# Two fewer steps in a reciprocal square root, scales found by integer steps, column sums accumulated in PSUM, and a new written order

## The chip, the cores and the metric

The kernel runs on one core of one Trainium2 chip, in one launch. The metric is the device time of that launch in microseconds (us). Lower is better. Five engines share the work, each with its own queue that is served in order: TensorE (PE) multiplies matrices, VectorE (DVE) and ScalarE (ACT) do elementwise work and reductions, GpSimd (POOL) builds a few constants at the start, and SyncE (SP) issues the transfers. An engine that reaches an instruction whose input is not there yet waits, and everything behind it on that engine waits too.

## The reference

The program is an attention layer followed by two layers of matrix products, all on 2304 tokens of width 512.

```python
scores = scale * np.matmul(q, k.transpose(0, 1, 3, 2))      # q, k, v: 4 x 8 x 576 x 64
mask_plain = (rel >= 0) & (rel < window)                    # heads 0 to 3, window 32
mask_dil = (rel >= 0) & (rel < window * dilation) & (rel % dilation == 0)   # heads 4 to 7
attn = softmax(np.where(masks, scores, -1e9)); x = np.matmul(attn, v)

h = x @ w_in                                                # 512 -> 1024
solu = h * softmax(h)
ln = (solu - mu) / np.sqrt(var + 1e-06) * g_ln              # mean and variance over the 1024
x = ln @ w_out                                              # 1024 -> 512

h = x @ w_in2                                               # 512 -> 2048
g = np.maximum(h, 0.0) + np.log1p(np.exp(-np.abs(h)))       # softplus
out = g @ w_out2                                            # 2048 -> 512
```

(`softmax` stands here for the reference's own lines: subtract the row's maximum, take the exponential, divide by the sum.)

## The kernel before

**Numbers as pairs.** Most products are made in 16-bit floats from operands that are split in a high and a low half, so one product of the reference is three on PE (high by high, high by low, low by high). Before a tensor is split it is scaled by a power of two that is near the root mean square of the whole tensor. There are 14 such scales: one each for the two weights of the first layer (`w1i`, `w1o`), one for each quarter of the two weights of the second (`w2i0` to `w2i3`, `w2o0` to `w2o3`), and one set of three (for q, k and v) for each of the four batches (`pre0` to `pre3`).

**How a scale is found.** ACT squares the tensor piece by piece and leaves one column of 128 partial sums per piece (8 pieces for a first-layer weight, 4 for a quarter, 9 columns for a batch, or 3 in `pre0`, which needs v alone). PE then multiplies a 128 x 128 matrix of ones in 32-bit floats by all those columns at once, which adds over the partitions. The operations of PE are named `w1im`, `w2o1m`, `pre1m` and so on. DVE adds the columns up (`tensor_reduce`), and the four steps of `scale_of` take the maximum with a tiny number, clear the mantissa by two shifts, take the reciprocal and multiply it. Only then can the tensor be split.

**The attention** goes through 28 pairs of blocks, `n` = 0 to 27, seven for each batch; the two blocks of a pair are written n.0 and n.1. The first ten pairs work in 32-bit floats and turn their operands on PE (`tq`, `tk`, `tp`, `tx`); the other eighteen work in split 16-bit floats and turn them by transposing transfers. In both, `QK` is the product of scores, `PV` the product with the values. Between `QK` and `PV` of a late block stand, in this order: the mask with its maximum on DVE (`mx`), four exponentials on ACT (`ex`), the split into high and low half (`ph`, `pl`), and a transposing transfer (`pT`).

**The first layer** has 18 tiles of 128 tokens. `m1a` and `m1b` are its products (12 each). Behind them a chain of DVE and ACT steps makes the gated and normalised tile. In that chain the reciprocal square root of the variance is found on DVE alone with numbers of one column (`m1k`): a first guess by integer steps on the bit pattern, and then refinements. Its result goes through a transposing transfer, and `ya`, `yb` multiply it by the second weight, 24 products each.

**The second layer** has, for each group of 256 tokens, eight products `h` (24 matrix products each) and eight products `o` (12 each), with the softplus between. The groups 5 to 8 are taken in two twins that save one product in eight by sums of the weights (operations `P`).

**What sets the order.** No scheduler decides it. Every operation is recorded with its engine choices, and a long table of numbers (`ORDER`) gives the sequence in which the operations are written out, with the engine of those that could run on either DVE or ACT; a second table (`SLOTS`) gives the buffers. A negative number in `ORDER` stands for a **fill**: a product of the unit matrix by itself into a PSUM bank that is free at that place, 128 x 512 in 16-bit floats, whose result nobody reads. The functions that the change touches are printed here with the line numbers of the profile. In them `ts`, `stt`, `recip` are DVE instructions on one or a few columns, `mm` is one product on PE, and `P.chain` records steps of which each waits for the one ahead.

Of the kernel before, what the change touches and what calls it, by code (L numbers as in the profile page):

```python
# [144 lines left out]
def kernel(  # L145
# [12 lines left out]
    nc = tc.nc  # L158
# [32 lines left out]
        65, 66, 247, 248, 278, 277, 0, 13, -2, -2, -2, 250, 252, 2943, 3, 2945, 14, 67, 69, -2, -2, 280, 254, 281,  # L191
        1, 255, 266, 267, 256, 15, 16, 4, 249, 68, -5, -5, -5, -5, -5, -5, -5, 257, 5, 279, 282, 6, 28, 308, 18,
        70, 268, 2, -5, -5, -5, 71, 7, 2975, 2950, 269, 307, 72, 73, 74, 75, 76, 77, 78, -5, 284, 309, 285, 296,
        -5, 259, 270, 17, 260, 286, -5, -5, -5, 287, 288, 261, 29, 2954, 263, 264, 297, 271, 272, 310, 33, 30,
        2965, -5, -5, -5, -5, 313, 38, 274, -5, 298, 367, 314, 299, 19, 20, 31, 32, -5, -5, 315, 275, 21, 22, 3008,
        289, 290, 276, 265, 34, 35, 291, 23, -5, -5, -5, -5, 317, 300, 366, 292, -5, -5, 293, 36, 318, 319, 37,
        301, 39, 40, 302, 41, 303, -5, -5, -5, -5, -5, 320, 321, 294, 24, 25, 26, 8, -5, -5, -5, -5, 304, 305, 42,
        9, 10, 11, -5, 372, 365, 306, 329, 27, 295, 373, 364, 79, 80, 12, -5, -5, -5, -5, -5, -5, -5, -5, -5, -5,
        -5, -5, -5, -5, -5, 43, 44, 45, 46, 311, 368, 312, 47, 48, 330, 81, 2753, 82, 370, 371, 53, 49, -5, -5, -5,
        331, 51, 62, 332, 421, 83, -5, 374, -5, -5, -5, 424, 425, 54, 94, 375, 422, 376, 63, 114, 322, 386, 95,  # L200
        323, 50, 52, -5, 333, 64, 334, -5, -5, 377, 324, 387, 378, -5, -5, -5, -5, -5, -5, 388, 96, 3017, 451, 84,
        426, 369, 59, 389, 115, 109, 423, 427, -5, -5, -5, 326, 97, 335, 60, 57, 327, 428, 336, 328, -5, -5, 337,
        379, 429, 440, 452, 380, 116, 507, 55, 98, 338, 339, 430, 381, -5, -5, -5, -5, -5, -5, -5, 431, 382, 454,
        117, 1163, 56, 432, 110, -5, 383, 58, -5, 433, 142, 99, 111, 112, 85, 455, 390, 118, 441, 508, 384, 391,
        385, 89, 505, 434, 86, 340, 435, 100, 442, 87, 113, 443, 101, 88, 341, 392, 393, 394, 102, 90, 91, 104,
        444, 92, 445, 103, 456, 436, 342, 395, 457, 93, 506, 105, 397, 343, 143, 106, 396, 446, 234, 562, 107, 511,
        437, 344, 347, 144, 513, 398, 512, 345, 563, 453, 438, 439, 108, 346, 458, 235, 447, 448, 177, 145, 348,
        146, 514, 147, 349, 399, 153, 459, 470, 565, 449, 566, 178, 218, 158, 350, 179, 450, 879, 481, 180, 460,
        461, 509, 471, 119, 351, 154, 181, 352, 462, -4, -4, 472, 567, 568, 219, 148, 400, 353, 120, 354, 155, 463,
        355, 121, 356, 156, 357, 122, 464, 358, 157, 465, 473, 515, 474, 159, 359, 160, 123, 232, 360, 220, 161,  # L210
        516, 527, 162, 124, 3053, 517, 518, 149, 125, 3158, 2820, 150, 2828, 475, 528, 233, 529, 129, 151, 519,
        140, 530, 2818, 476, 221, 878, 467, 362, 881, 882, 510, 520, 182, 477, 152, 222, 908, 521, 183, 883, 522,
        184, 132, 884, 224, 187, 478, 479, 3215, 223, 468, -1, 524, 185, 141, 480, 525, 526, 531, 186, 401, 137,
        469, 532, 130, 225, 138, 569, 133, 402, 533, 363, 403, 134, 404, 570, 188, 163, 581, 164, 571, 131, 189,
        226, 165, 139, 405, 582, -6, -6, -6, -6, -6, 583, 572, 534, 535, 135, 192, 909, 228, 227, 230, 910, 127,
        406, 482, 573, 536, 564, 166, 190, 914, 167, 407, 193, 911, 191, 168, 408, 194, 409, 195, 410, 175, 176,
        229, 411, 537, 196, 197, 592, 231, 412, 483, 413, 171, 880, 169, 538, 198, 414, 199, 584, 415, 1160, 173,
        1164, 200, 172, 201, 170, 236, 416, 174, 915, 237, 484, 202, 238, 885, 593, 239, 886, 240, 594, 417, 916,
        597, 203, 418, 241, 595, 539, 242, 917, 1161, 897, 243, 419, 244, 204, 887, 888, 245, 596, 205, 598, 206,
        599, 898, -3, -3, -3, -3, -3, 574, 207, 485, 585, 575, 208, 576, 889, 577, 486, 600, 607, 899, -1, -1, -1,  # L220
        -1, 578, 586, 1171, 209, 487, 587, 588, 488, 601, 900, -1, -1, -1, -1, -1, -1, 589, 579, 1172, 608, 420,
        489, 609, 890, 590, 591, 891, 580, 210, 602, 214, 216, 892, 610, 901, 902, 912, -5, -5, 971, 893, 211, 894,
        903, 611, 490, 1205, 895, 215, 1162, 540, 904, 212, 603, 491, 604, 217, 1212, 605, 492, 896, 213, 972, 606,
        905, 906, 907, 973, 626, 627, 493, 1159, -5, -5, -5, -5, -5, -5, 612, 613, 974, 913, 494, 631, 628, 614,
        495, 629, -5, -5, -5, 918, 496, 919, 497, 615, 967, 930, 616, 498, 617, 246, 499, 630, 3314, 541, 500, 632,
# [1524 lines left out]
```

## Time and profile before

| what | value |
|---|---|
| median of 3 runs | 697.88 us (694.92 to 698.5) |
| the profiled execution | 698.44 us, of which 696.5 us lie between the first and the last instruction (the span) |
| PE busy | 675.2 us, 97% of the span |
| DVE busy | 556.0 us, 80% |
| ACT busy | 480.9 us, 69% |
| mean granted clock of PE | 0.988 of full speed |

The busy share of PE counts fills as work, and the ends of its matrix products are modelled, so one product's duration overlaps the next one's. What a product costs in a row of many is therefore read from the distance between two starts, not from its duration. The shares over the whole span mix two very different stretches: in the first 130 us or so the weights are being split and the attention's first pairs are made, by DVE and ACT above all, and after that there is always a matrix product ready for PE.

### The profile page before, as it was taken

Reading aid. Unit: us, or ns where it says so; the run is one execution under the profiler, and the core shown is the slowest. Engines: PE = TensorE matmul, PEld = TensorE weight load, DVE = VectorE, ACT = ScalarE, POOL = GpSimd, SP = SyncE. Lnnn points to the kernel's source line nnn. Section 1 sums busy time; section 2 is a strip of 40 time slices with the busy share of each in tenths; the row PEclk is TensorE's granted clock in tenths of the full one; section 3 lists DMA queues with packets and bytes.
Section 4 is the critical chain, followed back from the end, with each engine's and each line's share of the span. In section 5 each row is a group of like instructions: output and inputs, shape, how many; then the busy total and the mean of one; then the engine's idle time right before and its main releaser. Section 6 shows DMA issues by size and latency. Waiting matters only on the chain.

```text
span 696.5 us, 14184 instructions
## 1 busy us (share of the span) xinstructions
PE 675.2 (97%) x5223; PEld 463.9 (67%) x5223; DVE 556.0 (80%) x1619; ACT 480.9 (69%) x1015; POOL 3.5 (1%) x22
## 2 busy tenths in 40 slices
PE   7999699999999999999999999999999999999997
PEld 4665547766765588688667668666776668676653
DVE  4999999999999968788889899887887768544233
ACT  4889998999998776987799797976364632322312
POOL 2000000000000000000000000000000000000000
PEclk9999689999999999999999999999999999999999
DMA  9889987669876558989887887652012110000001
GB/s 266 247 233 259 225 225 193 162 170 188 184 147 164 146 176 185 200 162 157 158 152 153 153 162 136 116 113 43 1 31 62 31 31 1 1 32 31 1 1 60
DMA packets 186773, 89.80 MB, mean 129 GB/s; under 512 B 157000, under 2 KB 174416, under 8 KB 186704
## 3 DMA queue, kind: packets, MB, share of 16 engines
q1 hardware_dynamic: 186704, 88.90, 56.4%
q8 instruction: 41, 0.67, 0.4%
q14 instruction: 28, 0.23, 0.1%
HBM read 54.53 MB, written 4.72 MB: 85 GB/s over the span
## 4 chain that ended last, share of the span: by engine, by line
PE 69%; DVE 12%; DMA 10%; ACT 4%; issue 3%; SPq 1%; ACTq 0%; DVEq 0%
PE ps_w L552 31%; PE bank L552 26%; PE bank L1550 11%; DMA xd<-x 2%; DVE E L543 2%; DMA E<-in_v_dram 2%; DMA qT<-qk 1%; DMA pT<-p 1%; DVE W L543 1%; PE bank L558 1%; DVE s L1122 1%; DMA W<-in_moe_w_out_dram 1%; ACT E L534 1%; DMA rv<-in_v_dram 1%; DMA rq<-in_q_dram 1%
## 5 line engine op out<-in xcount | busy, mean ns | idle before, releaser
L552 PE MATMUL ps_w<-W,g 128*128 128x512 f16 x864 | 194.3, 379 | 0.0
L552 PEld LDWEIGHTS <-W 128*128 128x128 f16 x1824 | 176.5, 98 | 23.3 <-DMA lnT<-hl 0.7
L552 PEld LDWEIGHTS <-g 128*128 128x128 f16 x864 | 83.6, 98 | 91.4
L552 PE MATMUL bank<-y,W 128*128 128x256 f16 x960 | 109.9, 273 | 0.0
L552 PE MATMUL ps_w<-W,xr 128*128 128x512 f16 x432 | 99.5, 382 | 1.0 <-ACT xr L534 1.0
L552 PE MATMUL bank<-lnT,W 128*128 128x256 f16 x864 | 98.7, 273 | 0.2 <-DMA lnT<-hl 0.2
L552 PEld LDWEIGHTS <-xr 128*128 128x128 f16 x432 | 42.1, 99 | 46.9 <-ACT xr L534 1.5
L543 DVE SCALAR_TENSOR_TENSOR g<-r,KR,g 128x512 f16<-128x512 f32 x68 | 50.3, 744 | 15.2 <-ACT g L534 14.2
L1718 ACT ACT_TABLE_LOAD x43 | 55.2, 1283 | 0.7
L1550 PEld LDWEIGHTS <-W 128*128 128x128 f16 x480 | 47.0, 98 | 8.4
L534 ACT ACTIVATE E<-E 128x768 f32<-128x768 f32 (+3 forms) x51 | 37.9, 744 | 15.7 <-DVE E L543 8.8
L534 ACT ACTIVATE s<-s 96x128 f32<-96x128 f32 (+3 forms) x144 | 43.5, 374 | 2.4 <-DVE st L538 1.2
L1122 DVE CUSTOM_DVE_ANT_0 s<-bank,band,bsc 96x128 f32<-96x128 f32 (+3 forms) x144 | 38.9, 324 | 3.9 <-PE bank L552 3.6
L534 ACT ACTIVATE r<-bank,invC 128x512 f32<-128x512 f32 x40 | 27.2, 685 | 16.4 <-PE bank L552 15.5
L534 ACT ACTIVATE r<-r,invT 128x512 f32<-128x512 f32 x21 | 14.6, 714 | 32.5 <-DVE r L546 32.4
L534 ACT ACTIVATE xf<-bank,rs 80x64 f32<-80x64 f32 (+1 forms) x128 | 29.3, 314 | 7.2 <-DVE rs L549 4.8
L552 PE MATMUL ps_w<-eye 128*128 128x512 bf16 x108 | 31.4, 407 | 0.7 <-DVE e L543 0.7
L534 ACT ACTIVATE g<-r,KR 128x512 f16<-128x512 f32 x35 | 24.9, 715 | 6.6 <-PE ps_w L552 6.3
L552 PEld LDWEIGHTS <-pT 128*96 128x96 f16 (+3 forms) x432 | 23.1, 123 | 6.9 <-issue 1.5
L543 DVE SCALAR_TENSOR_TENSOR E<-E 128x512 int32<-128x512 int32 x40 | 27.1, 683 | 0.1
L552 PEld LDWEIGHTS <-eye 128*128 128x128 bf16 (+2 forms) x162 | 16.5, 111 | 15.8 <-POOL eye L611 4.0
L534 ACT ACTIVATE hl<-e,st 128x1024 f16<-128x1024 f32 x18 | 22.3, 1242 | 5.4 <-DMA lnT<-hl 3.2
(295 smaller groups left out, 1102.9 us busy)
## 6 DMA issues: line engine op xcount, KB each, us to landing
E<-in_moe_w_in_dram SPq DMA_DIRECT2D x17, 512.0 KB, 4.8
E<-in_moe_w_out_dram SPq DMA_DIRECT2D x17, 512.0 KB, 4.1
out_dram<-osb SPq DMA_DIRECT2D x18, 256.0 KB, 2.4
W<-in_moe_w_in_dram SPq DMA_DIRECT2D x7, 512.0 KB, 5.7
W<-in_moe_w_out_dram SPq DMA_DIRECT2D x7, 512.0 KB, 6.2
E<-in_v_dram SPq DMA_DIRECT2D x9, 384.0 KB, 4.0
E<-in_q_dram SPq DMA_DIRECT2D x9, 384.0 KB, 3.4
E<-in_k_dram SPq DMA_DIRECT2D x9, 384.0 KB, 3.4
```

The costliest lines, as they stand in the source:

```text
L534: pin(nc.scalar.activation(out=out, in_=in_, func=func, **kw))
L543: pin(nc.vector.scalar_tensor_tensor(out=out, in0=in0, scalar=s, in1=in1, op0=op0, op1=op1, **kw))
L552: pin(nc.tensor.matmul(out, l, r, start=start, stop=stop))
L558: pin(nc.tensor.transpose(out, in_, eye32[:in_.shape[0], :in_.shape[0]]))
L1122: pin(nc.vector.tensor_tensor_reduce(out=sv()[:rows, h, :nk], in0=sb.t[:rows, h, :nk], in1=band[:rows, 48 - m:48 - m + nk], scale=sc[:rows ...
L1550: pin(nc.tensor.matmul(ps.t[:, ff, :], at(w, cc, ff), yo.t[:, v, cc, :], start=start, stop=cc == 1 and x == 2, skip_group_check=True,))
L1718: pin(nc.scalar.preload_act_table_set(TABLES[tab]))
```

## The change

There are four parts.

1. **The chain of the root.** The nine one-column steps become seven, in each of the 18 tiles. The first guess is one instruction (a multiplication of the integer by -0.5 and an addition) where it was two, and three refinements of two instructions each become one of three and one of two.
2. **The scales.** The columns of partial sums are no longer multiplied by the ones in one product and then added on DVE. PE makes one 32-bit product with the ones for each column (three for a batch) and accumulates them in PSUM. DVE's `tensor_reduce` goes, and so do the reciprocal and the multiplication, for which one integer step stands (a subtraction of exponents).
3. **Small leftovers.** A copy in each batch's scale, a negative scale that nobody reads, and three of four one-column doublings go.
4. **The order.** `ORDER` and `SLOTS` are new throughout. The four PSUM banks are four separate tiles in both kernels.

```diff
     ORDER = (
-        65, 66, 247, 248, 278, 277, 0, 13, -2, -2, -2, 250, 252, 2943, 3, 2945, 14, 67, 69, -2, -2, 280, 254, 281,
+        232, 236, 231, 234, 235, 63, 64, 261, -2, -2, 264, 265, 2855, 238, 0, 1, 239, 250, 2620, 240, 233, 262, 13,
...
-    def scale_of(inv, sc, ss):
+    def scale_of(inv, sc, ss, uses):
 
         i = sc.bitcast(INT32)
         return [
-            (TINY, lambda e: ts(sc, ss() if callable(ss) else ss, 2.0 ** -80, op0=ALU.max)),
+            (dve_cost(0, x=1), lambda e: ts(sc, ss(), 2.0 ** -80, op0=ALU.max), [], uses),
             (TINY, lambda e: ts(i, i, 24, 23, ALU.logical_shift_right, ALU.logical_shift_left)),
-            (TINY, lambda e: recip(inv, sc)),
-            (TINY, lambda e: ts(inv, inv, 2.0 ** -50)),
+            (TINY, lambda e: ts(inv.bitcast(INT32), i, -1.0, float((254 - 50) << 23), ALU.mult, ALU.add)),
         ]
...
-        m = P.op(f"pre{b}m", pe_cost(0.15), lambda e: mm(pb.t[:, 3 * c0:9], ones, am[:, 3 * c0:9], True, True), after=parts, uses=[pb])
...
+        def total(e):
+            for x in range(3):
+                mm(pb.t[:, c0:3], ones, am[:, 3 * c0 + x:9:3], x == 0, x == 3 - 1)
+
+        m = P.op(f"pre{b}m", pe_cost(0.2), total, after=parts, uses=[pb])
...
         pb = Buf(ps_x)
-        m = P.op(f"{name}m", pe_cost(0.15), lambda e: mm(pb.t[:, 0:n], ones, am[:, 0:n], True, True), after=squares, uses=[pb])
+        cols = list(range(n))
+
+        def total(e):
+            for i in cols:
+                mm(pb.t[:, 0:1], ones, am[:, i:i + 1], i == cols[0], i == cols[-1])
+
+        m = P.op(f"{name}m", pe_cost(0.06 + 0.06 * len(cols)), total, after=squares, uses=[pb])
...
-            (TINY, lambda e: pin(nc.vector.tensor_reduce(out=t[:, 0:1], in_=pb.t[:, 0:n], axis=AXX, op=ALU.add)), [], [pb]),
-            *scale_of(inv, sc, t[:, 0:1]),
+            *scale_of(inv, sc, lambda: pb.t[:, 0:1], [pb]),
...
             lambda e: ts(col(7), col(6), 1.0 / F1, 1e-6, ALU.mult, ALU.add),
-            lambda e: ts(i32(9), i32(7), 1, op0=ALU.logical_shift_right),
-            lambda e: ts(i32(9), i32(9), -1.0, float(0x5F3759DF - 2 ** 31), ALU.mult, ALU.add),
+            lambda e: ts(i32(9), i32(7), -0.5, float(0x5F3759DF - 2 ** 31), ALU.mult, ALU.add),
             lambda e: stt(col(10), col(9), col(9), col(7), ALU.mult, ALU.mult),
-            lambda e: stt(col(9), col(10), 3.0, col(9), ALU.subtract, ALU.mult),
+            lambda e: stt(col(8), col(10), 10.0 / 3.0, col(10), ALU.subtract, ALU.mult),
+            lambda e: stt(col(9), col(8), 5.0, col(9), ALU.add, ALU.mult),
             lambda e: stt(col(10), col(9), col(9), col(7), ALU.mult, ALU.mult),
-            lambda e: stt(col(9), col(10), 12.0, col(9), ALU.subtract, ALU.mult),
-            lambda e: stt(col(10), col(9), col(9), col(7), ALU.mult, ALU.mult),
-            lambda e: stt(col(10), col(10), 768.0, col(9), ALU.subtract, ALU.mult),
+            lambda e: stt(col(10), col(10), 64.0 / 3.0, col(9), ALU.subtract, ALU.mult),
```

**Where the order moves, on PE, at the sum of a quarter's squares.** The place is `w2o1m`, the sum for the second quarter of the last weight, some 134 us into the span. `amw_83` holds the columns of partial sums, `bank_137` the result, `y` and `xr` are the operands of the products ahead and behind. Before:

```order
947 L552 MATMUL bank_139<-y_123,W 128x256
948 L552 LDWEIGHTS eye
949 L552 MATMUL ps_w_140<-eye 128x512
950 L552 MATMUL bank_137<-amw_83,ones 128x4
951 L552 LDWEIGHTS xr
952 L552 MATMUL ps_w_140<-W,xr 128x512
```

The same place after:

```order
925 L547 MATMUL bank_139<-y_123,W 128x256
926 L547 LDWEIGHTS eye
927 L547 MATMUL ps_w_140<-eye 128x512
928 L547 MATMUL bank_137<-amw_83,ones 128x1 x4
929 L547 LDWEIGHTS xr
930 L547 MATMUL ps_w_140<-W,xr 128x512
```

One product of four columns has become four products of one column; the fill ahead of it and the first-layer tile behind it stand where they stood. The same happens at the other 13 sums. Counted over the whole order, the products with the ones go from 14 to 60, and the fills from 142 to 127.

**On DVE, at the last scale.** `s2o` is the scale of the last quarter, `tmp_91`, `invC`, `invD`, `iD` and `KR` are the factors made from it. Before:

```order
618 L738 TENSOR_REDUCE tmp_90<-bank_137 128x1
619 L538 TENSOR_SCALAR s2o<-tmp_90 128x1
620 L540 TENSOR_SCALAR s2o<-s2o 128x1
621 L549 RECIPROCAL s2o<-s2o 128x1
622 L538 TENSOR_SCALAR s2o<-s2o 128x1
623 L543 SCALAR_TENSOR_TENSOR invC<-s2i,s1o 128x1
```

After:

```order
566 L533 TENSOR_SCALAR s2o<-bank_137 128x1
567 L535 TENSOR_SCALAR s2o<-s2o 128x1 x2
568 L538 SCALAR_TENSOR_TENSOR invC<-s2i,s1o 128x1
569 L535 TENSOR_SCALAR tmp_91<-invC 128x1
570 L538 SCALAR_TENSOR_TENSOR tmp_91<-tmp_91,s2o 128x1
```

Five instructions have become three, the first of them reading PSUM.

**On PE, in the middle of the attention, ahead of `PV21.0`.** `pT` is the transposed matrix of weights that the transfer brings, `v` the values; `lnT` by `W` is `ya4.1`. Before, the 24 products of `ya4.1` stand between the scores of pair 22 (`kT`) and `PV21.0`; the first and the last of them are shown here:

```order
5067 L552 MATMUL bank_136<-kT,qT 80x80
5068 L552 LDWEIGHTS W
5069 L552 MATMUL bank_138<-lnT_122,W 128x256
...
5114 L552 LDWEIGHTS W
5115 L552 MATMUL bank_138<-lnT_122,W 128x256
5116 L552 LDWEIGHTS pT
5117 L552 MATMUL bank_137<-v_111,pT 80x65
```

After:

```order
5036 L547 LDWEIGHTS E
5037 L547 MATMUL bank_136<-kT,E 80x80
5038 L547 LDWEIGHTS pT
5039 L547 MATMUL bank_137<-v_111,pT 80x65
...
5061 L547 MATMUL bank_137<-v_111,pT 80x65
5062 L547 LDWEIGHTS W
5063 L547 MATMUL bank_139<-lnT_122,W 128x256
```

`PV21.0` now follows the scores directly, and `ya4.1` comes behind it.

## Rows read from the trace of the kernel before

**Rows 1.** Busy time by stretch: engine busy (instructions), granted PE clock, DMA share, GB/s.
```profile
5.00:64.00 59.00, 58.76 (x450) 37.61 (x449) 53.32 (x130) 45.93 (x149) 0.00 (x0) 1.00 0.95 259
64.00:72.00 8.00, 7.05 (x61) 4.40 (x59) 7.41 (x29) 8.00 (x23) 0.00 (x0) 1.00 0.83 259
72.00:94.00 22.00, 15.59 (x86) 10.44 (x86) 20.61 (x56) 20.84 (x62) 0.00 (x0) 0.61 0.97 241
94.00:131.00 37.00, 35.80 (x299) 25.86 (x298) 35.65 (x118) 33.20 (x93) 0.00 (x0) 1.00 0.74 184
131.00:300.00 169.00, 167.49 (x1311) 116.26 (x1309) 152.64 (x477) 146.15 (x297) 0.00 (x0) 1.00 0.74 172
300.00:430.00 130.00, 127.48 (x1155) 93.53 (x1154) 114.33 (x420) 108.92 (x203) 0.00 (x0) 1.00 0.83 155
430.00:683.00 253.00, 253.00 (x1830) 171.70 (x1828) 168.61 (x391) 115.21 (x194) 0.00 (x0) 1.00 0.18 38
```

**Rows 2.** Who PE waited for from 131 us on: us in total, times, longest.
```profile
PE bank L552 <- DMA pT<-p: 1.0, 1, 1.0
PE ps_w L552 <- ACT xr L534: 1.0, 1, 1.0
PE bank L552 <- DMA qT<-qk: 0.9, 2, 0.5
PE bank L552 <- DVE xf L546: 0.5, 1, 0.5
PE bank L552 <- ACT xf L534: 0.4, 1, 0.4
```

**Rows 3.** Groups by line and shape, the fills: count, busy us, mean ns, idle before.
```profile
L552 PE MATMUL ps_w<-eye 128*128 128x512 bf16 x108 | 31.4, 407 | 0.7 <-DVE e L543 0.7
L552 PE MATMUL bank<-eye 128*128 128x512 bf16 x34 | 10.8, 421 | 4.9 <-POOL eye L611 4.0 <-ACT qk L534 0.9
```

**Rows 4.** Chain that ended last, one piece, fifteen fills: start us, us, what.
```profile
29.58 3.24 PE ps_w L552 x15
```

**Rows 5.** The tile of ones: duration ns min/median/max, first and last start, forms.
```profile
L552 PEld LDWEIGHTS bank<-amw,ones x20: 186/190/333, 32.4 to 238.2; 128*128 128x128 f32 x20
L552 PE MATMUL bank<-amw,ones x20: 169/253/373, 32.7 to 238.3; 128*128 128x4 f32 x16, 128*128 128x8 f32 x4
L552 PE MATMUL bank<-am,ones x8: 168/214/257, 15.3 to 315.5; 128*128 128x9 f32 x6, 128*128 128x3 f32 x2
```

**Rows 6.** PE and its weight loads in order of time, around two sums: start, us.
```profile
134.53 0.30 PEld L552 LDWEIGHTS bank<-amw,ones 128*128 128x128 f32 x2 [0.21 <-ACT E L534]
238.25 0.28 PE L552 MATMUL bank<-amw,ones 128*128 128x4 f32 x2
238.39 1.24 PE L552 MATMUL ps_w<-W,xr 128*128 128x512 f16 x5
```

**Rows 7.** PE in order of time, a 32-bit `PV` and the fill behind it.
```profile
126.11 0.82 PE L552 MATMUL bank<-xd,pT 96*96 96x65 f32 x8
126.76 1.03 PE L552 MATMUL ps_w<-eye 128*128 128x512 bf16 x4
128.49 2.78 PE L552 MATMUL bank<-y,W 128*128 128x256 f16 x24
```

**Rows 8.** DVE in order of time, the first and last of six, five of them one-column.
```profile
67.15 0.15 DVE L540 TENSOR_SCALAR st<-st 128x1 int32<-128x1 int32 x1
...
67.67 0.68 DVE L543 SCALAR_TENSOR_TENSOR W<-E,W 128x512 int32<-128x512 int32 x1
```

**Rows 9.** PE in order of time, the scores of block 21.0, `ya4.1` and `PV21.0`.
```profile
368.29 0.47 PE L552 MATMUL bank<-kT,E 128*80 128x80 f16 x8
389.51 2.79 PE L552 MATMUL bank<-lnT,W 128*128 128x256 f16 x24
393.32 0.65 PE L552 MATMUL bank<-v,pT 80*80 80x65 f16 x12 [1.03 <-DMA pT<-p]
```

More of the change, by code (lines that the diff above doesn't have):

```diff
@@ L655, in prepass @@
         pb = Buf(ps_x)
-        m = P.op(f"pre{b}m", pe_cost(0.15), lambda e: mm(pb.t[:, 3 * c0:9], ones, am[:, 3 * c0:9], True, True), after=parts, uses=[pb])
-        ss, qs, o = tmp[0], tmp[1], bsc[b]
+        def total(e):
+            for x in range(3):
+                mm(pb.t[:, c0:3], ones, am[:, 3 * c0 + x:9:3], x == 0, x == 3 - 1)
+        m = P.op(f"pre{b}m", pe_cost(0.2), total, after=parts, uses=[pb])
+        qs, o = tmp[1], bsc[b]
         batch_ok.append(P.chain(f"pre{b}e", [
-            (TINY, lambda e: pin(nc.vector.tensor_reduce(out=ss[:, c0:3], in_=pb.t[:, 3 * c0:9].rearrange("p (a b) -> p a b", b=3), axis=AXX, op=ALU.add)), [m], [pb]),
-            *scale_of(o[:, c0:3], qs[:, c0:3], ss[:, c0:3]),
+            *scale_of(o[:, c0:3], qs[:, c0:3], lambda: pb.t[:, c0:3], [pb]),
             *([] if c0 else [
                 (TINY, lambda e: stt(o[:, 3:4], qs[:, 0:1], 2.0 ** 97, qs[:, 1:2], ALU.mult, ALU.mult)),
-                (TINY, lambda e: stt(o[:, 6:7], qs[:, 0:1], -2.0 ** 97, qs[:, 1:2], ALU.mult, ALU.mult)),
             ]),
-            (TINY, lambda e: pin(nc.vector.tensor_copy(o[:, 5:6], qs[:, 2:3]))),
             (TINY, lambda e: ts(o[:, 7:8], qs[:, 2:3], 2.0 ** 50)),
-        ], after=batch_ok[-1:]))
+        ], after=[m, *batch_ok[-1:]]))
     def to_f32(dst, src):
@@ L793, in batch_scale @@
     def batch_scale(b):
-        stt(bsc[b][:, 4:5], bsc[b][:, 5:6], 2.0 ** 100, s1i[:, 1:2], ALU.mult, ALU.mult)
+        stt(bsc[b][:, 4:5], bsc[b][:, 7:8], 2.0 ** 50, s1i[:, 1:2], ALU.mult, ALU.mult)
     iv_ok = []
@@ L825, in w2_quarter @@
             lambda e: stt(KR0[:, c], s2o[:, 1, c], 2.0 ** 50, t[:, 1:2], ALU.mult, ALU.mult),
-            lambda e: ts(invT[:, c], invC[:, c], 2.0),
         )]
@@ L831, in w2_quarter @@
                 lambda e: recip(t[:, 2:3], iD),
+                lambda e: ts(invT, invC, 2.0),
                 lambda e: ts(KR, s2o[:, 1], 2.0 ** 50, t[:, 2:3], ALU.mult, ALU.mult),
@@ L1262, in m1 @@
             lambda e: ts(col(7), col(6), 1.0 / F1, 1e-6, ALU.mult, ALU.add),
[L1263 to L1264 removed]
+            lambda e: ts(i32(9), i32(7), -0.5, float(0x5F3759DF - 2 ** 31), ALU.mult, ALU.add),
             lambda e: stt(col(10), col(9), col(9), col(7), ALU.mult, ALU.mult),
[L1266 removed]
+            lambda e: stt(col(8), col(10), 10.0 / 3.0, col(10), ALU.subtract, ALU.mult),
+            lambda e: stt(col(9), col(8), 5.0, col(9), ALU.add, ALU.mult),
             lambda e: stt(col(10), col(9), col(9), col(7), ALU.mult, ALU.mult),
[L1268 to L1270 removed]
+            lambda e: stt(col(10), col(10), 64.0 / 3.0, col(9), ALU.subtract, ALU.mult),
         )], after=[va], uses=[st])
[L1272 removed]
+        c1 = P.op(f"m1x{t}", TINY, lambda e: ts(st.t[:, 11:13], st.t[:, 4:6], col(10), 27.0, ALU.mult, ALU.mult), after=[cf], uses=[st])
         def norm(e):
```

2 lines of the change are left out of this document (removed), and 347 rows, old and new, of tables (ORDER, SLOTS).

## The prediction

> **What bounds the kernel now.** I read the table of stretches first [rows 1], because the shares over the whole span hide that there are two regimes. The reader is to see three things in it. From 5 to 64 us PE is busy for 58.76 of 59 us, so it never waits, but only because fills stand wherever nothing else is ready. From 64 to 94 us PE waits for 7.4 us (0.95 and 6.41), its granted clock falls to a mean of 0.61 from 72 us on, and DVE and ACT are busy for 28.0 and 28.8 of the 30 us: they set the pace. From 94 us on PE is full again. From 131 us it is busy for 167.49 of 169 us, then 127.48 of 130, then 253.00 of 253: what PE is given to do there is the time that passes, whereas DVE and ACT have slack that grows. Next come the waits of PE behind 131 us [rows 2]: five kinds and 3.8 us in all, so at most that much can be won there by faster steps on other engines. Last I read what one fill and one product with the ones cost, from distances between starts.
>
> So the change has to be judged by two sums: how much sooner PE comes to the point from which it is full (I take the first product of the second layer, at 128.49 us [rows 7]), and what it does behind that point.
>
> **The prices.** Fifteen fills in a row take 3.24 us, 0.216 us each [rows 4]; the group's mean durations of 407 and 421 ns [rows 3] overlap and are no price. A product with the ones is recorded as two weight loads and two multiplications: 20 of each for the ten sums of weights [rows 5]. Two loads of 0.19 us take 0.30 us together [rows 6], so the second starts 0.11 us behind the first, and a product inside a row of such products takes 0.22 us. This fits the 32-bit `PV`, eight multiplications of 96 columns in 0.65 us [rows 7], 0.081 us each, which for 128 columns is an estimate of 0.108 us. A product alone takes 0.14 us, from 238.25 to 238.39 [rows 6], since its first load hides beside the product ahead of it. A row of four therefore takes 0.14 + 3 x 0.22 = 0.80 us, and the width of the product (four columns, one column) hardly counts, since the load sets the pace. The Trainium skill (FP8 and Floating Point Precision, TensorE Precision Notes) says that a true 32-bit product goes four times through the array. The trace has two loads and two multiplications for each; by the rule the term below would be 8.4 us instead of 4.2 and the sum 704.5 us, and I go by the trace and give the rule no chance of its own.
>
> Five one-column steps of DVE go by in 0.52 us, from 67.15 to 67.67 [rows 8], so a step that goes is worth 0.10 us of DVE.
>
> **Behind 131 us.** Seven sums stand there: `w2o1`, `w2i2`, `w2o2`, `w2i3`, `w2o3` with three products more each and `pre2`, `pre3` with two more each. That is 19 products, 19 x 0.22 = 4.2 us, on an engine without slack. Of the fills, 14 stood behind the first `h` and 8 do now: 6 x 0.216 = 1.3 us less. The other products of PE are the same in number and shape. The one-column steps that go on DVE here (28 of the root chains, 20 others) lie beside PE's products: DVE is busy for 152.64 of 169 us, then less [rows 1], and they pay only where PE waits for them. That could take away all 4.0 us of idle time that rows 1 show between 131 and 430 us, or nothing; new waits could come as well, and the dearest that I can see in the order is 2.6 us (the first rival). I take nothing for the waits, because what PE waits for in rows 2 is transfers and wide steps, not one-column steps. Behind 430 us PE has no wait to lose, and the end (the last two products `o`, then two halves of the result on ACT and DVE) is as it was.
>
> **Ahead of 131 us.** From 5 to 64 us the sums of `pre0` and `w1i` get 2 and 7 more products, 9 x 0.22 = 2.0 us, and the fills ahead of the first tile go from 88 to 75, 13 x 0.216 = 2.8 us less. PE's work shrinks by 0.8 us. DVE (53.32 of 59) and ACT (45.93) are not far from full there, so I take half, -0.4 us. From 64 to 94 us DVE loses eight one-column steps (two each at `w1o`, `w2i0` and in two tiles), 0.8 us, and ACT, as full, loses none: half again, -0.4 us. PE gets 4.6 us more there (eleven fills more, 2.4, and ten products more, 2.2), beside its 7.4 us of idle time, so I cost it at nothing; if the clock is at half over all of it, it is 9.2 us, and 1.8 us stick out. From 94 to 131 us PE is nearly full: seven fills less (1.5) and eight products more (1.8), +0.3 us. Together -0.5 us. The ends: all 26 one-column steps that go ahead of 131 us count in full, -2.7 us, or the 1.8 us above.
>
> **The sum**, against the profiled execution's own 698.44 us: 698.44 - 0.5 + 4.2 - 1.3 = 700.8 us. The median of the runs shown is 0.56 us below that execution, and I predict medians, so 700.3 us. What a measurement of this kernel can tell from no change is about 0.5%, 3.5 us: faster is below 694.4, slower above 701.4.
>
> **Rival 1, slower: `PV21.0` comes too early.** Before, `PV21.0` had the scores of its block at 368.29, and PE reached it at 392.29 and then waited 1.03 us for its transposing transfer [rows 9]. The new order takes `ya4.1` from between, 24 products or 2.6 us (0.109 us each, from the start at 389.51 to 392.29 less the 0.16 us by which a modelled end overlaps). If mask, exponentials, split and transfer take as long as they did, the wait is 3.6 us and everything behind it on PE comes 2.6 us later; `PV20.0`, ahead of it, has lost cover too and would spend the same delay first. The time is 700.3 + 2.6 = 702.9 us. It decides as soon as DVE and ACT have not brought that block's split forward by 1.5 us, which is what is needed to stay under 701.4. For it: this wait was there already. Against it: the whole order of DVE is new as well, and DVE has fewer steps ahead of this block. Chance 0.20.
>
> **Rival 2, faster: the supply side decides all of it.** DVE's steps count in full ahead of 131 us (-2.7 instead of -0.5), and all idle time between 131 and 430 us goes (-4.0). That is 700.3 - 2.2 - 4.0 = 694.1 us. For it: DVE is busy for 35.65 of 37 us between 94 and 131 [rows 1]. Against it: so is PE, 35.80, and the waits of rows 2 are few and differ in kind. Chance 0.20.
>
> **Rival 3, slower: the clock falls sooner.** The granted clock is 1.00 as long as PE is kept busy, and 0.61 where it was busy for 15.59 of 22 us [rows 1]. Thirteen fills fewer ahead of the first tile could open such a stretch where PE was never idle. A second stretch like that of 72 to 94 us would take 0.39 x 22 = 8.6 us of PE's time; half of that, as an estimate, because the rest would have been idle, gives 700.3 + 4.3 = 704.6 us. Against it: more fills now stand between 64 and 95 us, where the clock did fall. The Trainium skill (TensorE: Matmul & The Clock Gate, HAM oscillation) says that a pause of PE between products throttles it and that the products behind the pause then run at half rate. The rows agree: 0.61 behind the first long waits. Chance 0.10.
>
> **Rival 4: the added products cost nothing.** At a sum PE may wait for the last square in any case: at 134.53 the load had waited 0.21 us for ACT [rows 6]. Then all products but the last could run inside that wait, and little is paid. If a quarter of the 4.2 us is left, the time is 700.3 - 3.2 = 697.1 us. Against it: at 238.25 there was no wait [rows 6], the squares being long done. Chance 0.12.
>
> **How the numbers follow.** The forecast has the remaining 0.38; its own range is 698 to 702 us. It and rival 4 lie within 0.5%, apart from an upper edge of the forecast (0.06). Most of rivals 1 and 3 is slower (0.25), and a good half of rival 2 faster (0.12); with a little for what I have not seen, faster 0.15, same 0.54, slower 0.31. The range goes from rival 2's 694.1 to rival 3's 704.6 us.
>
> **What would show it.** In the changed kernel's profile a sum of four columns must show eight multiplications with the ones, 0.11 us apart, with the next product about 0.8 us behind the first. If they come 0.06 us apart, or the next product starts as early as before, the term of 4.2 us is wrong. The first `h` must start between 126 and 130 us, with the clock at 1.00 up to 64 us and again from about 94. From there to 683 us or so PE must be full, with waits of about 4 us in all; a wait of over 2 us on `pT` near 390 us is rival 1, no wait at all rival 2. The prediction would be wrong above all if the new order changes the waits by more than 3 us in either direction, for that is what the rows before say least about.

## The result, and the profile of the changed kernel

| kernel | median | runs | lowest, highest |
|---|---|---|---|
| before, same chip | 698.13 us | 20 | 694.92, 700.41 |
| changed | 701.89 us | 20 | 697.55, 707.77 |

The ratio of the two is 1.0062, 95% interval 1.0041 to 1.0084: 4.3 us slower. The median lies 1.6 us above the forecast of 700.3 and just past 701.4, where the prediction let "slower" begin. A second measurement, e11 below, gave 1.0085 (1.0051 to 1.0119). The changed kernel also scatters over 10 us where the old one scatters over 5.5, and the profile that came with the first measurement is of its fastest execution, 697.55 us (span 695.8). That profile shows the mechanisms; for sizes I go by the ratios. One execution of e10 below took 1417.15 us, twice the others, and counts in no ratio.

Its table of stretches, the same columns as in [rows 1]:

```profile
5.00:64.00 59.00, 57.86 (x450) 38.17 (x450) 49.71 (x124) 46.41 (x147) 0.00 (x0) 1.00 0.90 251
64.00:72.00 8.00, 8.00 (x74) 6.00 (x72) 7.31 (x25) 6.95 (x23) 0.00 (x0) 1.00 0.79 235
72.00:94.00 22.00, 18.66 (x113) 12.86 (x111) 21.17 (x54) 22.00 (x67) 0.00 (x0) 0.69 0.89 262
94.00:131.00 37.00, 35.46 (x306) 26.99 (x305) 35.59 (x109) 34.10 (x95) 0.00 (x0) 1.00 0.68 181
131.00:300.00 169.00, 168.64 (x1329) 118.94 (x1328) 147.74 (x447) 144.89 (x287) 0.00 (x0) 1.00 0.77 170
300.00:430.00 130.00, 129.16 (x1171) 94.74 (x1169) 114.09 (x415) 105.57 (x209) 0.00 (x0) 1.00 0.81 154
430.00:683.00 253.00, 252.69 (x1830) 172.01 (x1829) 171.56 (x390) 105.45 (x172) 0.00 (x0) 1.00 0.18 40
```

DVE has less to do from 5 to 64 us (49.71 for 53.32) and from 131 to 300 us (147.74 for 152.64), as its shorter chains should give. In this table it buys PE nothing visible: PE is busy for 168.64 of 169 us and 129.16 of 130, fuller than before. From 64 to 72 us PE has no idle time left, where it had 0.95 us.

What PE waited for behind 131 us, the answer to [rows 2] (us in total, times, longest):

```profile
PE ps_w L547 <- ACT osb L529: 0.8, 1, 0.8
PE bank L547 <- DMA kT<-E: 0.3, 1, 0.3
PE bank L547 <- ACT E L529: 0.2, 1, 0.2
PE bank L547 <- ACT g L529: 0.2, 1, 0.2
```

1.5 us in place of 3.8, and no wait on `pT` any more. PE in order of time around `PV21.0`, which answers to [rows 9]:

```profile
387.64 2.78 PE L547 MATMUL bank<-lnT,W 128*128 128x256 f16 x24
390.26 0.47 PE L547 MATMUL bank<-kT,E 128*80 128x80 f16 x8
390.56 0.62 PE L547 MATMUL bank<-v,pT 80*80 80x65 f16 x12
391.02 5.19 PE L547 MATMUL bank<-lnT,W 128*128 128x256 f16 x46
```

`PV21.0` starts 0.30 us after the start of the products in front of it and waits for nothing. And two sums of four columns, in order of time, with the products behind them, for [rows 6]:

```profile
134.26 0.95 PE L547 MATMUL bank<-amw,ones 128*128 128x1 f32 x8
135.07 2.75 PE L547 MATMUL ps_w<-W,xr 128*128 128x512 f16 x12
...
238.10 0.95 PE L547 MATMUL bank<-amw,ones 128*128 128x1 f32 x8
238.91 2.32 PE L547 MATMUL ps_w<-W,xr 128*128 128x512 f16 x10
```

Eight multiplications each, and the next product starts 0.81 us behind the first; 0.14 us was the price of the one wide product.

### The profile page after: what moved, and what is told of

Its sections match the earlier page's. It is cut to its first block, busy times and chain, and to the rows that moved or that the text cites. A ratio compares the mean times of both kernels' runs of the same rounds, so it can differ in the third digit from the quotient of the medians.

```text
span 695.8 us, 14282 instructions
## 1 busy us (share of the span) xinstructions
PE 679.7 (98%) x5300; PEld 474.1 (68%) x5300; DVE 549.8 (79%) x1563; ACT 469.4 (67%) x998; POOL 3.5 (1%) x22
## 4 chain that ended last, share of the span: by engine, by line
PE 85%; DMA 6%; ACT 5%; DVE 3%; issue 1%; SPq 0%; ACTq 0%; DVEq 0%
PE ps_w L547 39%; PE bank L547 34%; PE bank L1547 11%; PE bank L553 2%; ACT E L529 1%; DMA lnT<-hl 1%; ACT W L529 1%; DMA W<-in_moe_w_out_dram 1%; DMA W<-in_q_dram 1%; DMA E<-in_moe_w_in_dram 1%; DMA qk<-in_v_dram 1%; DMA kT<-E 1%; DMA xd<-x 1%; DVE E L538 1%; ACT e L529 0%
## 5 line engine op out<-in xcount | busy, mean ns | idle before, releaser
L547 PE MATMUL ps_w<-W,xr 128*128 128x512 f16 x432 | 97.7, 380 | 0.8 <-ACT osb L529 0.8
L529 ACT ACTIVATE r<-bank,invT 128x512 f32<-128x512 f32 x7 | 4.8, 682 | 33.0 <-PE bank L1547 33.0
L533 DVE TENSOR_SCALAR g<-r,KR 128x512 f16<-128x512 f32 x32 | 15.4, 480 | 12.5 <-PE ps_w L547 9.7
```

The costliest lines, as they stand in the source:

```text
L529: pin(nc.scalar.activation(out=out, in_=in_, func=func, **kw))
L533: pin(nc.vector.tensor_scalar(out=out, in0=in0, scalar1=s1, scalar2=None, op0=op0))
L547: pin(nc.tensor.matmul(out, l, r, start=start, stop=stop))
```

## The experiments

Theory S: the added products are paid in PE's time, and the new order is neutral. The rivals are named with each group. Every ratio is to the kernel before on the same chip, from 5 rounds. "First `h`" is the start of the first product of the second layer in that kernel's one profile; it is 128.5 us before and 128.6 us in the changed kernel. e1 to e4 ran on one chip, e5 to e11 on another, e12 on a third. A profile is of one execution: up to the first `h`, e7 gives PE the same work as e1, and e6 the same as the changed kernel, and both start it 1.5 us later than their twin. So 1.5 us between two profiles says nothing by itself.

| kernel | ratio | 95% interval | first `h`, us |
|---|---|---|---|
| e1: new order, single products | 0.9965 | 0.9952 to 0.9979 | 126.0 |
| e2: old order, rows of products only | 1.0080 | 1.0068 to 1.0092 | 130.9 |
| e3: old order, all other parts | 1.0060 | 1.0046 to 1.0073 | 129.3 |
| e4: old order, only the shorter DVE steps | 0.9985 | 0.9970 to 1.0000 | 127.2 |
| e5: changed, single products ahead of 131 us | 0.9993 | 0.9976 to 1.0011 | 126.4 |
| e6: changed, single products behind 131 us | 1.0011 | 0.9991 to 1.0031 | 130.1 |
| e7: e1 without the fills behind the first `h` | 0.9964 | 0.9945 to 0.9984 | 127.5 |
| e8: changed, every row twice | 1.0333 | 1.0297 to 1.0370 | 142.9 |
| e9: changed, a fill for each product of a row | 1.0160 | 1.0136 to 1.0184 | 132.2 |
| e10: changed, single products at `w1i`, `w1o` | 1.0021 | 1.0000 to 1.0041 | 128.8 |
| e11: the changed kernel again | 1.0085 | 1.0051 to 1.0119 | 135.4 |
| e12: changed, single product at `pre0` | 1.0048 | 1.0028 to 1.0068 | 128.4 |

### Order or products: e1 to e4

e1 is the changed kernel with the one thing put back, at all 14 sums:

```diff
-            for i in cols:
-                mm(pb.t[:, 0:1], ones, am[:, i:i + 1], i == cols[0], i == cols[-1])
+            mm(pb.t[:, 0:n], ones, am[:, 0:n], True, True)
+
+        def summed():
+            t = tmp[2]
+            pin(nc.vector.tensor_reduce(out=t[:, 0:1], in_=pb.t[:, 0:n], axis=AXX, op=ALU.add))
+            return t[:, 0:1]
```

> The changed kernel, order and all, but each sum is again one product of all columns with the ones, and DVE adds the columns (14 reductions of 0.16 us come back). Theory S (the 19 products added behind 131 us are paid in full, 4.2 us, and the order is neutral): about 698 us, ratio to the kernel before 0.998 to 1.002, and the stretch behind the first h is about 4 us shorter than in the changed kernel. Theory O (the products run inside waits and the new order itself is what is slower): still 701 to 702 us, ratio 1.004 to 1.007.

e2 is the kernel before with rows of products in place of its 14 single ones (DVE's `tensor_reduce` stays, over one column), e3 the kernel before with parts 1 to 3 of the change and without the new order, e4 the kernel before with the shorter root chain, the integer scale step and the leftovers, but its single products. The integer step, as e3 and e4 have it (the other steps are those of the change):

```diff
-            (TINY, lambda e: recip(inv, sc)),
-            (TINY, lambda e: ts(inv, inv, 2.0 ** -50)),
+            (TINY, lambda e: ts(inv.bitcast(INT32), i, -1.0, float((254 - 50) << 23), ALU.mult, ALU.add)),
```

> The kernel before with its own order and all its DVE steps; only the sums are made by one product for each column, accumulated, so 46 products are added on PE and nothing else moves. Theory S: +4.2 us behind 131 us and up to 1 us ahead of it, 702 to 703 us, ratio 1.005 to 1.008. Theory O: the added products disappear in waits, ratio 0.999 to 1.002.

> The kernel before in its own order with all three parts of the change to the arithmetic (root chain of seven, integer scales, accumulated products, leftovers), fills as before; against the changed kernel only the order differs. Theory S: 4.2 us more on PE, less what shorter DVE chains give, 700 to 702 us, ratio 1.003 to 1.006, as the changed kernel. Theory O: at or below the kernel before, ratio 0.996 to 1.000.

> The kernel before in its own order with the shorter DVE steps alone (root chain of seven, one integer step for reciprocal and multiplication, leftovers); sums by one product and a reduction as before. It measures what the steps on DVE are worth by themselves: 60 one-column steps less, about 2.0 us of DVE ahead of 131 us. If they count in full there and shorten the waits later: 694 to 695 us, ratio 0.994 to 0.996. If they lie beside PE's work, as the prediction mostly took it: 697 to 698 us, ratio 0.998 to 1.000. Theories S and O do not differ on this one.

e2 alone is as slow as the whole change, 5.6 us with the old order. e1 without the rows is 2.4 us faster than before, and faster than the changed kernel by 0.0097, 6.8 us. The order makes no difference that can be told: 1.0062 against 1.0060 with all parts, 0.9965 against 0.9985 without the products. The shorter DVE steps bring 1.0 us, at the edge of what can be measured. By the ratios theory S holds and the rival (the order is slower) falls. S also had the stretch behind the first `h` about 4 us shorter in e1; it is 2.3 us shorter (564.8 for 567.2 us to the end of the span). The size is larger than S said: 5.6 and 6.8 us, not 4.2. The starts say where the rest is: in e2's profile the first `h` comes 2.4 us later than before, in the changed kernel 2.7 us later than in e1. The products ahead of 131 us, which I had hidden, cost something too.

### Ahead or behind: e5, e6, e10

The same edit as in e1, at the seven sums ahead of 131 us, at the seven behind, and at the two rows of eight.

> The changed kernel with one product and the reduction on DVE again for the seven sums ahead of 131 us (pre0, w1i, w1o, w2i0, w2o0, pre1, w2i1); the seven behind keep their rows of products. Theory S, a product of a row costs its 0.22 us of PE wherever PE has no idle time: only the 27 products ahead go, which in the profiles so far brought the first h 2.4 to 2.6 us later. Ratio to before 1.0062 - 0.0036 = 1.0026 (1.001 to 1.004), and the first h at 126 us. Rival F, what costs is that the scales ahead of 131 us come later, and the products behind lie beside waits: all of the gain comes back, ratio 0.9965 (0.995 to 0.998).

> The other half: one product and the reduction on DVE for the seven sums behind 131 us (w2o1, w2i2, w2o2, w2i3, w2o3, pre2, pre3), rows of products ahead. Theory S: 19 products go from a full PE, 19 x 0.22 = 4.2 us, ratio 1.0062 - 0.0060 = 1.0002 (0.999 to 1.002), the first h still at 128.6 us. Rival F: nothing or little comes back, ratio 1.005 to 1.007. Under theory S the parts of this run and of the one with the seven sums ahead add up to the difference between the changed kernel and the one with a single product everywhere, 0.0097.

> The changed kernel with one product and the reduction on DVE at the two longest rows alone (w1i and w1o, eight products each); 32 products more than before stay. Theory S, every added product ahead costs alike: 14 of the 27, so 14/27 of the 0.0069 that the one with seven single products ahead brought, ratio 1.0062 - 0.0036 = 1.0026 (1.0015 to 1.004). Theory C, the long rows cost more than their time, since the clock can fall behind them, and the short rows ahead of 131 us lie beside waits: nearly all of the 0.0069, ratio 0.999 to 1.001.

Behind: 1.0062 - 1.0011 = 0.0051, 3.6 us (1.5 to 5.6, the two intervals put together) for 19 products, 4.2 us expected. Ahead: 1.0062 - 0.9993 = 0.0069, 4.8 us (2.9 to 6.8) for 27 products, 2.5 expected from the profiles. Taken from e11, the changed kernel on the chip of e5 and e6, the two are 5.2 us (2.4 to 7.9) and 6.4 us (3.7 to 9.1). e6 is what S said, and rival F falls with it. e5 gave back more than the 1.001 to 1.004 of S and less than F asked for: most of the 5.9 us that the 27 products take on PE is paid, not two fifths of it. e10 lies between the two theories' numbers, nearer to S: 14 of the 27 products brought 0.0041 of the 0.0069. Against e11, measured beside it, they brought 0.0064, and its interval holds S's number and reaches C's, so e10 does not tell the two apart.

The profiles leave more open behind 131 us than the ratios do. From the first `h` to PE's last product e6 takes 562.7 us, just as long as the changed kernel; PE has 19 products less to do, but is idle for 4.8 us in place of 1.5. Most of that lies between 131 and 300 us, where the changed kernel's PE was busy for 168.64 us:

```profile
131.00:300.00 169.00, 166.15 (x1302) 115.66 (x1300) 149.94 (x455) 145.21 (x293) 0.00 (x0) 1.00 0.78 171
```

In all seven profiles that have the rows behind 131 us (the changed kernel, e2, e3, e5, e10, e11, e12; e8 and e9, with more in them, left aside) PE is idle for 0.7 to 3.5 us over that distance, in the five without (before, e1, e4, e6, e7) for 2.8 to 5.1 us. So a part of the added products seems to stand in time that PE would otherwise have waited. How large a part is not shown: the ratios have 3.6 us paid of 4.2, with an interval that reaches down to 1.5.

### More than PE's time: e8, e9

```diff
-            for i in cols:
+            for i in cols * 2:
                 mm(pb.t[:, 0:1], ones, am[:, i:i + 1], i == cols[0], i == cols[-1])
```

> The changed kernel with every row of products run twice, the second row starting its sum anew: 34 products more ahead of 131 us and 26 behind, no other change. Theory S: 26 x 0.22 = 5.7 us behind, and ahead the same share of the price as in the change itself (2.5 of 27 x 0.22 = 5.9 us), 3.2 us of 7.5: ratio 1.0062 + 8.9 / 698 = 1.019 (1.015 to 1.024), and a sum of four takes 7 x 0.22 + 0.14 = 1.7 us. Rival L, what a sum costs is not PE's time for a product but a wait of fixed length (for the reader of its bank): less than half of it, ratio under 1.012.

Slower than either theory had it: 1.0333 - 1.0062 = 0.0271, 18.9 us for 60 products that take 13.2 us of PE. More than their whole time is nothing that S can explain. The table of stretches around the first weight's row, which now has 16 products, and that row with its neighbours in order of time:

```profile
34.00:38.00 4.00, 3.97 (x35) 3.11 (x31) 2.91 (x6) 2.88 (x12) 0.00 (x0) 0.98 1.02 218
38.00:43.00 5.00, 5.00 (x24) 4.30 (x24) 1.49 (x4) 0.51 (x3) 0.00 (x0) 0.50 0.70 209
43.00:48.00 5.00, 5.00 (x29) 4.31 (x29) 3.65 (x10) 3.40 (x7) 0.00 (x0) 0.50 0.25 68
48.00:52.00 4.00, 4.00 (x37) 2.59 (x36) 2.73 (x8) 2.78 (x10) 0.00 (x0) 0.99 0.86 238
```

```profile
34.70 1.03 PE L547 MATMUL ps_w<-eye 128*128 128x512 bf16 x4
35.61 5.37 PE L547 MATMUL bank<-amw,ones 128*128 128x1 f32 x32
40.84 0.59 PE L547 MATMUL ps_w<-eye 128*128 128x512 bf16 x1
```

The granted clock falls to 0.50, the lower of PE's two levels (1.2 GHz), some two microseconds after the row began and stays there for ten microseconds, with PE busy all the time. The row takes 5.2 us instead of 3.4, and DVE and ACT, which wait for the scale, nearly stop (1.49 and 0.51 of 5 us). It is not this profile alone: the mean granted clock of the six executions of e8 is 0.969 to 0.982, that of the changed kernel's 20 is 0.979 to 0.990. But not every such row does it: behind the row of 16 at `w1o`, which starts at 73.29 us in the same profile, the clock stayed at 1.00 up to 84 us. To see whether it is these products or only the time that they fill, e9 puts fills of the same time in the place of the second row:

```diff
+            for _ in cols:
+                mm(pb.t, eye, eye.unsqueeze(1).broadcast_to([128, 4, 128]), True, True)
             for i in cols:
                 mm(pb.t[:, 0:1], ones, am[:, i:i + 1], i == cols[0], i == cols[-1])
```

> The changed kernel with 60 fills of 512 columns, 0.216 us each, ahead of the rows of products, one for each product of the row (eight ahead of w1i's row, and so on), where the kernel with the rows run twice has 60 products more of 0.22 us. Theory S, what the second rows cost is PE's time (PE is idle for 0.7 us in all ahead of the rows of the changed kernel): the same ratio as there, 1.030 to 1.036, and w1i's first tile again 7 us later than in the changed kernel. Theory C, a long row of one-column products also lets the clock fall (there it was 0.50 from 38 to 48 us, right behind w1i's row of 16, with PE busy all the time), and fills do not: granted clock 1.00 from 30 to 64 us, w1i's first tile 1.8 to 2.5 us later, ratio 1.018 to 1.026.

The table of stretches of e9 at the same place:

```profile
34.00:38.00 4.00, 4.00 (x28) 2.73 (x26) 1.63 (x4) 3.13 (x11) 0.00 (x0) 1.00 1.12 272
38.00:43.00 5.00, 5.00 (x44) 3.74 (x43) 4.69 (x14) 3.03 (x7) 0.00 (x0) 1.00 0.67 176
43.00:48.00 5.00, 5.00 (x50) 3.59 (x50) 5.00 (x13) 5.00 (x20) 0.00 (x0) 1.00 0.73 203
48.00:52.00 4.00, 4.00 (x33) 2.67 (x33) 3.92 (x10) 3.98 (x15) 0.00 (x0) 1.00 0.50 156
```

The clock stays at 1.00, and the first tile that waits for this scale starts at 50.99 us (49.8 in the changed kernel, 57.15 in e8). 60 fills, 13.0 us of PE, cost 0.0098, 6.8 us; the 60 products cost 12.1 us more than they (1.0333 - 1.0160). The ratio is below even the 1.018 that theory C gave as its least, and C holds in kind: a row of one-column products costs its time and can also take the clock away, and fills do not. The mean clock of e9's five executions is 0.987 to 0.995. As an estimate, one less the mean clock, times the span, is 17.5 us in e8 and 6.8 us in e9, so most of the 12.1 us is clock. A little of it is gained by the fills: from 72 to 94 us the clock is 0.84 in e9 and 0.69 in the changed kernel. Which property of the row does it (32-bit, one column, a load for each multiplication) no run separates. The Trainium skill (TensorE: Matmul & The Clock Gate, HAM oscillation) tells of a pause of PE as what throttles it. The trace of e8 differs: the clock fell with PE busy for 5.00 of 5 us, while it multiplied one column at a time.

Does it happen in rows of eight, as the change has them? In e6, whose PE does the same as in the changed kernel up to 134 us, it did, in the stretch behind the row of `w1o` (65.55 to 67.36 us):

```profile
64.00:68.00 4.00, 3.98 (x32) 2.86 (x30) 3.12 (x9) 4.00 (x14) 0.00 (x0) 1.00 0.76 225
68.00:72.00 4.00, 4.00 (x23) 2.35 (x22) 3.48 (x15) 2.58 (x9) 0.00 (x0) 0.57 0.65 195
```

The changed kernel's first profile has 1.00 there (the second row of the table of stretches above). There it costs 0.43 of 4 us, 1.7 us. Of the 14 rows of eight at `w1i` and `w1o` in the profiles of the changed kernel, e2, e3, e6, e9, e11 and e12 it is the only one with such a fall right behind it. Nor is the clock what made the change slower: the median of the mean granted clock is 0.987 over the changed kernel's 20 executions and 0.987 over the 18 of the kernel before that were measured beside e11.

### The scatter: e11, e12

> The changed kernel as it is, for a second profile and times on the chip of the other two: the first profile is of its fastest execution, 697.55 us, 4.3 us below its median. Theory S: a profile nearer to the median shows the same order of starts, with the 4 us more spread over small waits of PE ahead of 131 us, and the clock as before (0.50 from about 76 to 90 us). Theory C: it shows a further stretch at half clock behind one of the long rows (w1i's near 35, w1o's near 66 us), 5 us or more of it. Ratio to before 1.004 to 1.008 by both.

This execution took 705.94 us, and its first `h` starts 6.8 us later than in the first profile. Five of those are lost before the first weight's row begins (40.2 for 35.2 us). PE in order of time around the very first sum, first of the 697.55 us execution, then of this one:

```profile
12.65 1.91 PE L547 MATMUL ps_w<-eye 128*128 128x512 bf16 x4
14.35 0.90 PE L547 MATMUL bank<-am,ones 128*128 128x1 f32 x6
15.12 0.45 PE L547 MATMUL bank<-band,eye 80*80 80x320 bf16 x2
15.49 0.80 PE L547 MATMUL bank<-kT,qT 64*80 64x80 f32 x16
16.22 0.48 PE L553 MATMUL bank<-eye,s 80*80 80x80 f32 x4
16.53 1.03 PE L547 MATMUL ps_w<-eye 128*128 128x512 bf16 x4
```

```profile
12.77 1.91 PE L547 MATMUL ps_w<-eye 128*128 128x512 bf16 x4
14.47 1.28 PE L547 MATMUL bank<-am,ones 128*128 128x1 f32 x6
15.61 0.73 PE L547 MATMUL bank<-band,eye 80*80 80x320 bf16 x2
16.28 1.36 PE L547 MATMUL bank<-kT,qT 64*80 64x80 f32 x16
17.57 0.75 PE L553 MATMUL bank<-eye,s 80*80 80x80 f32 x4
18.11 1.91 PE L547 MATMUL ps_w<-eye 128*128 128x512 bf16 x4
```

Up to the sum the two are the same to 0.12 us, with PE at the lower rate (four fills take 1.91 us). In the first PE runs at full rate from the sum on (four fills 1.03 us). In the second the same products go on at half rate until about 25 us. Theory C's place, behind a long row, was wrong; what was late is the first rise of the clock, right where the three products of `pre0` stand. e12 takes those three away:

> The changed kernel with one product and the reduction on DVE at the first sum alone (pre0, near 14.4 us): two products fewer, one step of DVE more. In the second profile of the changed kernel PE went from the lower to the full rate only at about 25 us (four fills still took 1.71 us from 18.11), in the first one at 14.4 us, right at this row; the first weight's row started 5 us later there. Theory S, the row has nothing to do with that: 2 x 0.22 = 0.4 us, ratio 1.0056 to 1.008, and times as wide as those of the changed kernel (697.5 to 708.3 us over 27 executions). Theory C, the row of one-column products at that place is what makes the rise late: no execution above 704 us, and a ratio of 1.001 to 1.004.

Inconclusive. The times are narrower (699.05 to 702.72 us, 8 runs) and none is above 704, as theory C said; the ratio, 1.0048, is above the 1.004 that it allowed and below the 1.0056 of S, and its interval holds both. That the row of `pre0` makes the rise late is not shown, and the other profiles speak against it: in e2, e3, e6, e8 (with the row twice), e9 and e10, which all have the row, the fills behind it stand 0.22 us apart, the full rate. And e6, alike up to 134 us, has all 12 executions between 696.57 and 700.04 us. What made e11 late stays open.

### Are late fills worth their time: e7

```diff
+        seen = seen or isinstance(o, Op) and o.name == "h0.0"
         if not isinstance(o, Op):
+            if seen:
+                continue
```

> The changed kernel with one product and the reduction on DVE for all 14 sums, and without the eight fills that stand behind the first h in the order. Theory S, PE's time behind 131 us is what it is given to do: 8 x 0.216 = 1.7 us less than with the fills, ratio 0.9965 - 0.0025 = 0.994 (0.992 to 0.996). Rival W, the fills lie in waits of PE, or hold its clock up: no gain, ratio 0.9965 or above, and the same stretches show waits in their place or a granted clock below 1.00.

No gain: 0.9964 against 0.9965, though the two intervals together allow 1.7 us either way, and so just the gain that S expected. PE in order of time where six of the eight fills stood, e1 and then e7:

```profile
214.45 0.38 PE L547 MATMUL bank<-eye 128*128 128x512 bf16 x1
214.74 0.39 PE L547 MATMUL bank<-amw,ones 128*128 128x4 f32 x2
214.98 0.81 PE L547 MATMUL bank<-eye 128*128 128x512 bf16 x3
215.71 0.69 PE L547 MATMUL bank<-v,pT 128*96 128x65 f16 x12
216.23 0.60 PE L547 MATMUL bank<-eye 128*128 128x512 bf16 x2
216.93 5.34 PE L547 MATMUL ps_w<-W,g 128*128 128x512 f16 x24
```

```profile
216.91 0.39 PE L547 MATMUL bank<-amw,ones 128*128 128x4 f32 x2 [0.40 <-ACT E L529]
217.88 0.69 PE L547 MATMUL bank<-v,pT 128*96 128x65 f16 x12 [0.59 <-DVE tmp L739]
219.10 7.03 PE L547 MATMUL ps_w<-W,g 128*128 128x512 f16 x24 [0.54 <-DVE osb L538]
```

The fills stood in waits for ACT and DVE. Without them PE waits 1.5 us in three places, and the 24 products behind take 7.03 us instead of 5.34, because the granted clock falls (0.67 from 218 to 222 us, 1.00 in e1). Rival W holds in this profile, for that place.

## Why the prediction came out as it did

The forecast was 2.4 us slower (-0.5 + 4.2 - 1.3), the measured difference is 4.3. The side and most of the size come from the term of 4.2 us, which agrees with e6's ratio; the others were wrong and partly made up for each other, so it is in part luck that the sum came so near.

| term | predicted | the runs |
|---|---|---|
| 19 products more behind 131 us | +4.2 | +3.6 (1.5 to 5.6), e6 |
| six fills fewer behind 131 us | -1.3 | about 0: eight fewer bring 0.1 (1.7 either way), e7 |
| waits behind 131 us | 0 | from 3.8 to 1.5 us in the two first profiles |
| all ahead of 131 us | -0.5 | the 27 products alone +4.8 (2.9 to 6.8), e5 |
| DVE's shorter steps, whole kernel | inside the terms above | -1.0, e4 |
| the new order with its other fills | inside the terms above | -1.4 (0 to -2.8), e1 against e4 |
| all 46 products added | inside the terms above | +6.8 (5.0 to 8.6), e1 against the change |

The last three rows must add up to the difference, since each is one step from kernel to kernel (-1.0 - 1.4 + 6.8). e2's 5.6 us is a measure of the 46 products apart from them, with the old order. Of the 10.1 us that these take on PE, more than half is paid.

**The prices were right.** A product inside a row takes 0.22 us, a row of four 0.81 (0.80 predicted), and true 32-bit products go by two loads and two multiplications. The Trainium skill (FP8 and Floating Point Precision, TensorE Precision Notes) has a true 32-bit product go four times through the array. The 704.5 us that the prediction made of it took each pass to cost what a recorded load and multiplication cost; a row of four would then take twice its 0.81 us. The trace rules out that price, not the rule: whether each of the two multiplications recorded is two passes, a row of one-column products does not show.

**The step that failed** is the one that set products and fills against each other from 5 to 64 us: "PE's work shrinks by 0.8 us", halved to -0.4. The start of the first tile shows it, in the old order without and with the rows (before, e2), then in the new order (e1, the changed kernel):

```profile
48.87 2.75 PE L552 MATMUL ps_w<-W,xr 128*128 128x512 f16 x12
50.51 2.75 PE L552 MATMUL ps_w<-W,xr 128*128 128x512 f16 x12
47.99 2.75 PE L547 MATMUL ps_w<-W,xr 128*128 128x512 f16 x12
49.75 2.76 PE L547 MATMUL ps_w<-W,xr 128*128 128x512 f16 x12
```

The nine products added at `pre0` and `w1i`, 2.0 us by their price, bring it 1.6 us later in the old order and 1.8 us in the new one (1.8 also from e4 to e3), and 13 fills fewer do not give that back: the changed kernel comes 0.9 us later than the kernel before, where the term had it 0.4 us sooner. (e7, alike to e1 up to there, has 48.84 us, so a single difference is good to some 0.9 us.)

From 64 to 94 us "I cost it at nothing" held, so far as these profiles show: the sum of `w2i0` comes 2.0 us later in e2 than before (87.33 for 85.32) and 1.6 us later in the changed kernel than in e1 (85.05 for 83.41), little more or less than the first tile. But the delay from ahead of it is not given back in PE's idle time there: at the first `h` it is 2.4 us in e2 and 2.7 us from e1 to the changed kernel. DVE and ACT set the pace in that stretch and wait for the scales; that this is what passes the delay on is argued from the starts, not tested.

The ratios give 4.8 us for all 27 products, pairs of profiles 2.1 to 2.7. That can be chance, the interval starts at 2.9. The late rise in e11 (5 us) and the fall in e6 (1.7 us) would go the right way: with these two, the three profiles with all the rows ahead (the changed kernel, e6, e11) start the first `h` 4.8 us later in the mean than the three without (e1, e5, e7). How often either happens in the changed kernel, and whether the rows bring them on, the runs do not settle.

**The fills** were priced by their time on PE, as if nothing stood behind them. At the place that e7 shows, PE was busy only because of them; a fill is paid where the product behind it is ready. The six that the change takes away behind 131 us were not tested by themselves.

**The rivals.** Rival 1 did not come: `PV21.0` waits for nothing. Rival 2 had the waits behind 131 us go by faster steps on DVE. They did shrink, but in e1, e4, e6 and e7, which have the shorter steps and single products there, PE is idle for 2.8 to 5.1 us: it is where the rows stand that PE waits less. The shorter steps bring 1.0 us (e4). Rival 4, a quarter of the 4.2 us left, lies below the interval of e6 (1.5 to 5.6 us), but its mechanism, products inside waits, is in the profiles in part. Rival 3 had a clock that falls sooner, for want of fills; a fall was seen in e6 and e8, but behind one-column products and not where fills went, and in the mean the changed kernel's recorded clock is no lower; e11's late rise stays open.

## What to carry to other kernels

Price an instruction by what waits for its result, not only by the idle time of its own engine: the rows here came ahead of scales that DVE and ACT wait for, and the idle time that PE had further on did not make up for the delay. Moving a reduction from an engine with slack to the one without was a loss here, though it saves instructions; the version to keep is e1, the new order and the shorter DVE steps with the single product and the reduction on DVE, 0.9965 of the kernel before. Where a kernel scatters more after a change, take a second profile before explaining the median by the first.

## What was not expected of the hardware

- The granted clock fell to 0.50 behind 16 one-column 32-bit products in a row with PE busy for 5.00 of 5 us; with eight of them replaced by 512-column fills it stayed at 1.00. All six executions of the first kernel have a lower mean clock (0.969 to 0.982) than all five of the second (0.987 to 0.995).
- In two executions of one kernel, alike to 0.12 us up to 14.4 us, PE came to its full rate at 14.4 and at about 25 us. The granted clock is given as 1.00 from 5 us on in both; only the distance between fills (0.43 or 0.22 us) shows it.
- Fills taken out of waits of 1.5 us in all were followed by a fall of the clock, and 24 products then took 7.03 us instead of 5.34.
